# GpSimd takes over part of the scaling of v and of the block sums, and q, k and v get buffers of their own, in a retention layer followed by an MLP

## The chip, the core and the metric

The kernel runs on one core of a Trainium2 chip. The metric is device microseconds for one execution. The core's engines are TensorE (PE; PEld is its loading of weights), VectorE (DVE), ScalarE (ACT), GpSimd (POOL) and SyncE (SP), each of which works through its own list of instructions in order. Loads from memory are issued by GpSimd, stores and transposing copies by SyncE.

## The reference

For 8 sequences of 576 tokens and 8 heads of 64, scores of q and k are weighted by a decay that depends on the head and multiplied with v. The heads are laid side by side (4608 tokens of 512), and an MLP with exact GELU follows.

```
gamma = 1.0 - 2.0 ** (-5.0 - np.arange(H))
Dmat = np.where(rel >= 0, gamma[:, None, None] ** rel, 0.0)
x = matmul((matmul(q, k.T) / sqrt(64)) * Dmat, v)      # then to (B * S, H * D)
h = x @ w_in                                            # 512 -> 2048
g = 0.5 * h * (1.0 + erf(h / sqrt(2)))
out = g @ w_out                                         # 2048 -> 512
```

## The kernel before

**Retention.** The tokens are cut into 36 units of 128 tokens, numbered 0 to 35 (`units`, L138 on). Two sequences go together; a sequence has four chunks of 128 and a tail of 64, and the two tails share a unit. Units 0 to 3 are the first chunks of the first four sequences, and for them and some others v is also used as it was loaded. For each unit q, k and v are loaded (`load_unit`, L504), q and k are turned on PE (the first ten units) or by a transposing DMA (`turn_dma`, L603), PE makes the scores (sc), DVE masks them (ret), and PE multiplies with v scaled by the decay (vh). A running state in PSUM (u_ps, copied to u_sb) carries what earlier chunks contribute. DVE multiplies the result (o_ps) by the decay of the row (dqT) and writes it to x (tile xT, L843 and L855). `scaled_v` (L814) makes vh: on DVE as one product of v_ld with a broadcast of dv (L821), on ACT as eight activations, one for each head (L824). The list VH_ACT (L174) names the units for ACT; the rest go to DVE.

**MLP.** Nine blocks of 512 tokens, so four units each. w_in and w_out are loaded as eight tiles each (wi0 to wi7, wo0 to wo7). The first product goes through a block in four quarters. A quarter is either *plain* (16 matmuls with 512 columns) or a *unit of seven products* (28 matmuls with 256 columns, L1129): seven products of sums of blocks in place of eight products of blocks. LAYOUTS (L192) lists it for blocks 2 to 8: '0' is a unit of quarter 0, '12' two units whose products alternate, 'p3' a plain quarter, '1p2' a unit and a plain quarter that alternate. PRODUCTS (L199) is the order of the seven. A unit needs sums of x (xs, five for each block, `x_sum`, L1046 to 1054) and of w_in (wi_sum), and afterwards four DVE operations that put its quadrants together. In blocks 0 and 1 all is plain, block 0 in pieces of 128 columns. The second product is made of seven products in blocks 1 to 8 (`fast`, L1146) and needs sums of g (tiles s and g, four for each half of a block, `g_sum`, L989 to 999), numbered 0 to 3; the product called 6 needs sum 1, which needs sum 0.

**The order of the work.** No scheduler of the compiler is used. `Plan` (L30) holds operations with an engine, a duration, what they depend on, and a due time, and steps forward in planned time: on each engine it takes the operation that can start first, and among those within a little slack the one due first (`best`, L87). So the instructions of each engine are laid down in an order that is fixed at build time; on the chip only semaphores hold them. Matmul pieces of the MLP are taken from a window of LOOK pieces (L190) of the current product (`pe_candidates`, L1543), and the retention's work is put between them in groups ("macros", L1408); GAP_A, HOLD, APART, BEFORE, LEAD, SPREAD and EASE steer when. APART is read in ALONE (L874) and for groups from the fourth on. A change between tile shapes on PE costs some 0.09 us going in and 0.11 to 0.13 us coming out (start of the last matmul to start of the next, beyond a matmul's own pace).

**Loads.** GpSimd issues the loads in the order ORDER (L196; q3 is q of unit 3), then q, k and v unit by unit. A pair of units shares a slot: one tile for q and k, one for v, four slots in all (N_LD, L169; `tiles_of`, L475). `Ring` (L263) tells the plan when the next slot is free: it sorts the times at which slots were given back (`read`, L494). q, k and v of unit 0 come as float32 by SyncE and ACT. `warm` matmuls (L1515) keep PE busy in the first 16 us.

Of the kernel before, what the change touches and what calls it, by code (L numbers as in the profile page):

```python
# [29 lines left out]
class Plan:  # L30
# [4 lines left out]
    def __init__(self):  # L35
        self.ops = {}
        self.T = dict.fromkeys(self.ENGINES, 0.0)
        self.open = {e: [] for e in self.ENGINES}

# [42 lines left out]

    def start(self, op, engine):
        t = max(self.T[engine], op.ready)
        return max(t, op.at()) if op.at else t
# [13 lines left out]
    def run(self, op, engine, start):  # L99
        op.ran = engine  # L100
        self.T[engine] = self.T["now"] = start + self.dur(op, engine)
        if op.fn:
            op.fn(engine) if op.engine == "any" else op.fn()
        self.done(op, self.T[engine])
# [3 lines left out]
def kernel(  # L108
# [52 lines left out]
    def slot_of(i):  # L161
# [7 lines left out]
    N_LD = 4  # L169
# [4 lines left out]
    VH_ACT = [5, 8, 12, 14, 15, 17, 19, 20, 26, 28, 30, 31, 32, 35, 37]  # L174
# [10 lines left out]
    GAP_A = 4.2  # L185
    GAP_B = 1.5
    APART = [3, 6, 7]
    BEFORE = 0.4
    UNIT_FROM = 2
    LOOK = 16  # L190
    HOLD = 4.6
    LAYOUTS = {2: ['0', '12', 'p3'], 3: ['01', '2', 'p3'], 4: ['2', '30', 'p1'], 5: ['01', '2', 'p3'], 6: ['10', '2', 'p3'], 7: ['01', '23'], 8: ['3', '20', 'p1']}  # L192
    LEAD = 8
    SPREAD = 7.1
    EASE = 6.5
    ORDER = ("q3 q2 k3 q1 pos v2 k2 wi0 k1 wi4 v3 v1 wi1 wi3 wi5 v4 wi2 wi6 k4 wi7 q4 wo0 q5 k5 v5 wo4 wo1 q9 q8 "  # L196
             "wo5 v7 wo6 k7 wo7 v10 wo2 q6 v6 k6 wo3 q7 k10 q10 k8 k9 v9 v8").split()
    K_ORDER = [0, 1, 8, 9, 2, 3, 10, 11, 4, 5, 12, 13, 6, 7, 14, 15]
    PRODUCTS = "3251647"  # L199
# [6 lines left out]
    ld_pool = ctx.enter_context(tc.tile_pool(name="ld", bufs=N_LD))  # L206
# [56 lines left out]
    class Ring:  # L263
        def __init__(self, size):
            self.size, self.taken, self.free = size, 0, []

        def at(self):
            n = self.taken - self.size
            return 0.0 if n < 0 else (sorted(w.end + 0.12 if isinstance(w, Landing) else w for w in self.free)[n] if n < len(self.free) else NEVER)

        def take(self):
            self.taken += 1

        def give(self, when):
            self.free.append(when)

    ld_ring, tr_ring, vh_ring, ret_ring, x_ring = Ring(N_LD), Ring(N_QKT), Ring(N_VH), Ring(N_RET), Ring(3)
# [194 lines left out]
    loaded, slots, w_in_sb, w_out_sb = {}, {}, {}, {}  # L472
    touched = {}

    def tiles_of(i):  # L475

        if i not in loaded:
            n = slot_of(i)
            if i in kept:
                loaded[i] = (const.tile([128, 2, H, D], BF16, name=f"qk_ld{i}"), const.tile([128, H, D], BF16, name=f"v_ld{i}"))  # L480
                return loaded[i]
            if n not in slots:
                ld_ring.take()
                slots[n] = (ld_pool.tile([128, 2, H, 2, D], BF16, tag="qk", name="qk_ld"),
                            ld_pool.tile([128, 2, H, D], BF16, tag="v", name="v_ld"))
            qk, v_ld = slots[n]
            j = units[i][2] or 0
            if i in old:
                loaded[i] = (qk.rearrange("p a (j h) b d -> p j a (h b) d", j=2)[:, j], v_ld[:, j])
            else:  # L490
                loaded[i] = (qk[:, :, :, j], v_ld[:, j])
        return loaded[i]

    def read(i, what):  # L494

        n = slot_of(i)
        got = touched.setdefault(n, set())
        got.add((i, what))
        want = {(m, x) for m in pair_with(i) for x in
                ["v"] + (["turn0", "turn1"] if i < N_PE_TR else ["turn"]) + (["state"] if units[i][1] < NCI - 1 else []) + (["inner"] if i in raw else [])}  # L500
# [1158 lines left out]
```

## Time and profile before

| what | value |
|---|---|
| runs of the kernel before | median 283.02 us (282.54 to 283.83, 3 runs) |
| the profiled execution | 282.72 us, of which the span is 280.7 us |
| granted TensorE clock | 1.00 |
| DVE, ACT, POOL busy | 230.1, 174.0, 110.4 us |
| first matmul of the MLP's first product without warm matmuls behind it | 15.81 us |
| last matmul ends | 276.1 us |

The span runs from the first instruction to the last; some 2 us lie around it. In the page's second part each digit is the busy share of a fortieth of the span, in tenths. A row of instructions names the line, engine, operation and tiles (out<-in), the shapes, the count, then busy time and mean ns of one, then how long the engine sat idle before them and what ended it. A duration contains the tail in which the next instruction has already begun: DVE operations of 0.69 us start 0.60 us apart when nothing holds them. Of the waits the columns are: who waited for whom, us in total, times, the longest. In a timeline the columns are start, duration (of the merged run of instructions), engine, line, operation, tiles and count.

### The profile page before, as it was taken

To read this page: it belongs to the slowest core of one execution; us is meant where nothing else is said; L and a number is where in the kernel's file an instruction comes from. 1 tells how busy PE (TensorE), PEld (TensorE's weight loads), DVE (VectorE), ACT (ScalarE), POOL (GpSimd) and SP (SyncE) were. 2 spreads that over 40 slices of the span, in tenths; PEclk is the share of its full clock that TensorE was granted. 3 is DMA by queue.
4 is the path that set the end of the run, shared out by engine and by line. 5 is a ranking of instruction groups with operands and counts; after the bars stand their busy time and mean duration, and the time that the engine had idled before them with its cause. 6 is when DMAs were issued, how large, how long until landed. Compare 5 with 4: busy or idle time off the path is not lost.

```text
span 280.7 us, 8896 instructions
## 1 busy us (share of the span) xinstructions
PE 273.9 (98%) x3731; PEld 220.0 (78%) x3731; DVE 230.1 (82%) x438; ACT 174.0 (62%) x414; POOL 110.4 (39%) x139
## 2 busy tenths in 40 slices
PE   7999999999999999999999999999999999999993
PEld 2679767578888688868887888688868888888782
DVE  5870465699999998999799999987987799969832
ACT  7678733646438952995297319852898379528740
POOL 8967778847546086233326804705000000000000
PEclk9999999999999999999999999999999999999999
DMA  9999999999999999999989999999800040022013
GB/s 148 165 182 186 178 186 165 142 238 133 127 139 173 197 114 128 140 230 145 156 188 57 134 112 172 210 117 135 184 22 2 6 149 2 4 75 77 0 40 112
DMA packets 152071, 35.57 MB, mean 127 GB/s; under 512 B 141024, under 2 KB 147680, under 8 KB 152032
## 3 DMA queue, kind: packets, MB, share of 16 engines
q0 software_dynamic: 115792, 17.97, 98.1%
q1 hardware_dynamic: 35200, 16.78, 34.9%
q8 instruction: 29, 0.48, 0.8%
q10 hardware_dynamic: 1040, 0.26, 0.4%
q14 instruction: 10, 0.08, 0.1%
HBM read 36.70 MB, written 9.44 MB: 164 GB/s over the span
## 4 chain that ended last, share of the span: by engine, by line
PE 87%; DVE 4%; POOL 4%; DMA 3%; issue 1%; ACT 0%; POOLq 0%; DVEq 0%
PE oT L229 39%; PE hT L229 16%; PE zT L229 10%; PE yT L229 7%; PE o_ps L229 4%; DMA w_in<-in_moe_w_in_dram 3%; PE sc L229 2%; POOL qk_ld L517 2%; PE u_ps L229 2%; DVE s L999 1%; PE qk_ps L233 1%; DVE ret L652 1%; POOL v_ld L517 1%; POOL w_in L523 1%; DVE g L999 0%
## 5 line engine op out<-in xcount | busy, mean ns | idle before, releaser
L229 PEld LDWEIGHTS <-g 128*128 128x128 bf16 x576 | 55.1, 98 | 12.5 <-issue 0.2
L229 PEld LDWEIGHTS <-w_in 128*128 128x128 bf16 x656 | 53.0, 98 | 13.3 <-DMA w_in<-in_moe_w_in_dram 0.4
L229 PE MATMUL hT<-xT,w_in 128*128 128x128 bf16 (+2 forms) x480 | 53.5, 266 | 0.3 <-DMA w_in<-in_moe_w_in_dram 0.3
L229 PEld LDWEIGHTS <-wi_sum 128*128 128x128 bf16 x440 | 42.8, 98 | 6.6
L1099 ACT ACTIVATE g<-hT 128x512 bf16<-128x512 f32 (+1 forms) x72 | 35.9, 505 | 19.5 <-PE hT L229 17.7
L229 PE MATMUL oT<-w_out,g 128*128 128x256 bf16 (+1 forms) x320 | 45.6, 294 | 0.0
L517 POOL DMA_DIRECT2D qk_ld<-in_q_dram x31 | 28.0, 905 | 35.1 <-DMA qkT<-qk_ld 22.8
L229 PEld LDWEIGHTS <-s 128*128 128x128 bf16 x384 | 36.8, 98 | 5.6 <-DVE s L999 0.5
L517 POOL DMA_DIRECT2D v_ld<-in_v_dram x31 | 28.1, 910 | 22.8 <-ACT vh L824 9.5
L229 PE MATMUL oT<-w_sum,s 128*128 128x256 bf16 x256 | 32.4, 273 | 0.2 <-ACT o_sb L1243 0.2
L824 ACT ACTIVATE vh<-v_ld,dv 128x64 bf16<-128x64 bf16 x112 | 31.2, 346 | 1.0 <-DMA v_ld<-in_v_dram 1.0
L229 PE MATMUL oT<-w_sum,g 128*128 128x256 bf16 x256 | 30.8, 273 | 0.0
L517 POOL DMA_DIRECT2D qk_ld<-in_k_dram x31 | 28.0, 903 | 5.5 <-DMA v_ld<-in_v_dram 5.2
L1243 ACT COPY o_sb<-oT 128x512 f32<-128x512 f32 (+1 forms) x27 | 14.5, 538 | 25.2 <-PE oT L229 13.3
L1212 ACT ACTIVATE g<-zT 128x512 bf16<-128x512 f32 x44 | 25.9, 614 | 0.1
L652 DVE TENSOR_TENSOR ret<-sc,msk 128x512 bf16<-128x512 f32 x36 | 23.2, 687 | 1.4 <-PE sc L229 1.4
L1247 DVE TENSOR_TENSOR o_sb<-o_sb,oT 128x512 f32<-128x512 f32 (+1 forms) x27 | 16.8, 629 | 8.8 <-PE oT L229 4.5
L570 ACT COPY q<-yT 128x512 f32<-128x512 f32 x18 | 10.3, 594 | 21.8 <-PE yT L229 21.8
L855 DVE TENSOR_TENSOR xT<-o_ps,dqT 128x512 bf16<-128x512 f32 x26 | 16.8, 686 | 3.3 <-PE o_ps L229 3.3
L821 DVE TENSOR_TENSOR vh<-v_ld,dv 128x512 bf16<-128x512 bf16 x22 | 15.0, 688 | 3.4 <-DMA v_ld<-in_v_dram 3.4
L1221 DVE TENSOR_TENSOR zT<-q,zT 128x512 f32<-128x512 f32 x22 | 15.3, 695 | 1.0 <-PE zT L229 0.6
L1191 DVE TENSOR_TENSOR q<-q,zT 128x512 f32<-128x512 f32 x22 | 14.5, 684 | 1.7 <-PE zT L229 0.8
(170 smaller groups left out, 453.6 us busy)
## 6 DMA issues: line engine op xcount, KB each, us to landing
out_dram<-o_sb SPq DMA_DIRECT2D x30, 256.0 KB, 3.9
qk_ld<-in_q_dram POOLq DMA_DIRECT2D x31, 128.0 KB, 7.6
qk_ld<-in_k_dram POOLq DMA_DIRECT2D x31, 128.0 KB, 8.5
v_ld<-in_v_dram POOLq DMA_DIRECT2D x31, 128.0 KB, 8.0
w_in<-in_moe_w_in_dram POOLq DMA_DIRECT2D x8, 256.0 KB, 8.6
w_out<-in_moe_w_out_dram POOLq DMA_DIRECT2D x8, 256.0 KB, 7.8
out_dram<-o_sb SPq DMA_DIRECT2D x12, 128.0 KB, 2.7
v_ld<-in_v_dram POOLq DMA_DIRECT2D x8, 64.0 KB, 6.4
```

The source lines that it names most:

```text
L229: return nc.tensor.matmul(*args, **more)
L517: nc.gpsimd.dma_start(dst, src[2 * bp + j, :, ci * C:ci * C + C, :].rearrange("h s d -> s h d"))
L652: nc.vector.tensor_tensor(r, t, by, op=ALU.mult)
L821: nc.vector.tensor_tensor(vh, loaded[i][1], dv[:, :, ci:ci + 1].to_broadcast([128, H, D]), op=ALU.mult)
L824: nc.scalar.activation(vh[:, h], loaded[i][1][:, h], AF.Copy, scale=dv[:, h, ci:ci + 1])
L855: nc.vector.tensor_tensor(dst, o, dqT[:, :, ci * C:ci * C + C], op=ALU.mult)
L1099: nc.scalar.activation(g_of(t, m0)[:, m0 % 2:m0 % 2 + n, m0 // 8, lo:hi], hT, AF.Gelu)
L1191: nc.vector.tensor_tensor(q_, q_, chain[key]["Z"][1], op=ALU.subtract)
L1212: nc.scalar.activation(target(key, what), chain[key][n][1], AF.Gelu)
L1221: nc.vector.tensor_tensor(to, chain[key]["q"], z, op=ALU.add)
L1243: nc.scalar.copy(target(key, what), chain[key][n][1])
L1247: nc.vector.tensor_tensor(to, to, chain[key][n][1], op=ALU.add)
```

## The change

- `scaled_v` can run on GpSimd, as the same tensor product as on DVE. VH_POOL lists 19 numbers for it, VH_ACT shrinks from 15 to 4.
- XS_POOL lists 21 of the sums of x (block * 5 + number of the sum) and GS_POOL 20 of the sums of g (block * 8 + half * 4 + number) for GpSimd. The plan counts 1.1 us for v and for a sum of x there, 2.1 us for a sum of g, and a signal that is 0.25 us late (0.12 on DVE).
- The plan lets those operations with two inputs in SBUF (PAIR) of DVE and GpSimd start only when the other engine's last one has ended. This shapes the order alone; nothing on the chip waits for it.
- q, k and v have pools of their own with 3, 5 and 4 slots. A slot of q is given back when q is turned, one of k when the state has read it too. The ring follows the slot that is handed out next, in turn, rather than the first that comes free.
- The parameters of the order are others: the layouts (21 units of seven products and 7 plain quarters in blocks 2 to 8; before 22 and 6), the order of the products and of the loads, and the numbers that steer the groups.

The core of the diff (`read` and the lines that only pass on the new names are left out):

```diff
--- before.py
+++ after.py
@@ -36,6 +36,7 @@
         self.ops = {}
         self.T = dict.fromkeys(self.ENGINES, 0.0)
         self.open = {e: [] for e in self.ENGINES}
+        self.port = {"dve": 0.0, "pool": 0.0}
...
+    PAIR = ("vh", "gs", "xs", "ui", "ws", "dq")
+
     def start(self, op, engine):
         t = max(self.T[engine], op.ready)
+        if engine in self.port and op.name.startswith(self.PAIR):
+            t = max(t, self.port["pool" if engine == "dve" else "dve"])
         return max(t, op.at()) if op.at else t
 
...
+        if engine in self.port and op.name.startswith(self.PAIR):
+            self.port[engine] = self.T[engine]
...
-    N_LD = 4
+    N_LD = {"q": 3, "k": 5, "v": 4}
...
-    VH_ACT = [5, 8, 12, 14, 15, 17, 19, 20, 26, 28, 30, 31, 32, 35, 37]
+    VH_ACT = [8, 12, 22, 23]
+    VH_POOL = [5, 6, 7, 10, 13, 14, 15, 17, 18, 19, 20, 24, 28, 29, 31, 33, 34, 35, 37]
+    XS_POOL = [10, 13, 15, 18, 19, 23, 25, 26, 28, 29, 30, 31, 32, 33, 34, 35, 39, 40, 41, 42, 43]
+    GS_POOL = [18, 24, 25, 27, 33, 36, 39, 45, 46, 48, 49, 52, 53, 56, 57, 58, 63, 65, 67, 71]
     HOT = 10.1
     N_WARM = 8
     SLACK = 0.3
...
-    GAP_A = 4.2
+    GAP_A = 1.0
     GAP_B = 1.5
-    APART = [3, 6, 7]
-    BEFORE = 0.4
+    APART = [6, 7]
+    BEFORE = 0
     UNIT_FROM = 2
-    LOOK = 16
-    HOLD = 4.6
-    LAYOUTS = {2: ['0', '12', 'p3'], 3: ['01', '2', 'p3'], 4: ['2', '30', 'p1'], 5: ['01', '2', 'p3'], 6: ['10', '2', 'p3'], 7: ['01', '23'], 8: ['3', '20', 'p1']}
+    LOOK = 14
+    HOLD = 2.2
+    LAYOUTS = {2: ['2', '30', 'p1'], 3: ['0', '1p2', 'p3'], 4: ['01', 'p2', 'p3'], 5: ['01', '2', 'p3'], 6: ['01', '23'], 7: ['01', '23'], 8: ['0', '1', '2', 'p3']}
     LEAD = 8
-    SPREAD = 7.1
-    EASE = 6.5
-    ORDER = ("q3 q2 k3 q1 pos v2 k2 wi0 k1 wi4 v3 v1 wi1 wi3 wi5 v4 wi2 wi6 k4 wi7 q4 wo0 q5 k5 v5 wo4 wo1 q9 q8 "
-             "wo5 v7 wo6 k7 wo7 v10 wo2 q6 v6 k6 wo3 q7 k10 q10 k8 k9 v9 v8").split()
+    SPREAD = 7.5
+    EASE = 9
+    ORDER = ("pos q2 q3 k2 q1 k3 k1 v2 v3 wi0 v1 wi4 wi1 wi5 wi2 v4 wi6 wi3 wo0 q4 wi7 q5 k5 k4 v5 wo4 v7 wo1 wo5 "
+             "v6 wo6 k6 v10 wo7 k7 q7 wo2 q9 wo3 q6 q8 k10 q10 k9 k8 v9 v8").split()
     K_ORDER = [0, 1, 8, 9, 2, 3, 10, 11, 4, 5, 12, 13, 6, 7, 14, 15]
-    PRODUCTS = "3251647"
+    PRODUCTS = "3251476"
     SECOND = "1267534"
     LAYOUT = {t: ["p0", "p1", "p2", "p3"] for t in range(2, N_BLK)}
     for t in range(UNIT_FROM, N_BLK):
         LAYOUT[t] = LAYOUTS[t]
...
-            self.size, self.taken, self.free = size, 0, []
+            self.size, self.taken, self.free = size, [], {}
 
         def at(self):
-            n = self.taken - self.size
-            return 0.0 if n < 0 else (sorted(w.end + 0.12 if isinstance(w, Landing) else w for w in self.free)[n] if n < len(self.free) else NEVER)
-
-        def take(self):
-            self.taken += 1
-
-        def give(self, when):
-            self.free.append(when)
-
-    ld_ring, tr_ring, vh_ring, ret_ring, x_ring = Ring(N_LD), Ring(N_QKT), Ring(N_VH), Ring(N_RET), Ring(3)
+            n = len(self.taken) - self.size
+            w = self.free.get(self.taken[n], NEVER) if n >= 0 else 0.0
+            return w.end + 0.12 if isinstance(w, Landing) else w
+
+        def take(self, key=None):
+            self.taken.append(len(self.taken) if key is None else key)
+
+        def give(self, when, key=None):
+            self.free[len(self.free) if key is None else key] = when
+
+    ld_ring = {what: Ring(N_LD[what]) for what in "qkv"}
+    tr_ring, vh_ring, ret_ring, x_ring = Ring(N_QKT), Ring(N_VH), Ring(N_RET), Ring(3)
...
+    def slot_for(what, i):
+
+        n = slot_of(i)
+        if (what, n) not in slots:
+            ld_ring[what].take(n)
+            slots[what, n] = ld_pool.tile([128, 2, H, D] if what == "v" else [128, H, 2, D], BF16, tag=what, name=f"{what}_ld", bufs=N_LD[what])
+        return slots[what, n]
+
+    def loaded(what, i):
+
+        if i in kept:
+            if (what, i) not in slots:
+                slots[what, i] = const.tile([128, H, D], BF16, name=f"{what}_ld{i}")
+            return slots[what, i]
+        t, j = slot_for(what, i), units[i][2] or 0
+        if what == "v":
+            return t[:, j]
+        if i in old:
+            return t.rearrange("p (j h) b d -> p j (h b) d", j=2)[:, j]
+        return t[:, :, j]
+
...
-            def fits(i=i):
-                return max(room_to_fly(), 0.0 if i in kept or slot_of(i) in slots else ld_ring.at())
+            def fits(what=what, i=i):
+                return max(room_to_fly(), 0.0 if i in kept or (what, slot_of(i)) in slots else ld_ring[what].at())
...
     def scaled_v(i, engine, heads=(0, H)):
         ci = units[i][1]
         if "vh" not in st[i]:
-            vh_ring.take()
+            vh_ring.take(i)
             st[i]["vh"] = vh_pool.tile([128, H, D], BF16, tag="vh", name="vh")
         vh = st[i]["vh"]
-        if engine == "dve":
-            nc.vector.tensor_tensor(vh, loaded[i][1], dv[:, :, ci:ci + 1].to_broadcast([128, H, D]), op=ALU.mult)
+        if engine != "act":
+            (nc.vector if engine == "dve" else nc.gpsimd).tensor_tensor(
+                vh, loaded("v", i), dv[:, :, ci:ci + 1].to_broadcast([128, H, D]), op=ALU.mult)
         else:
             for h in range(*heads):
-                nc.scalar.activation(vh[:, h], loaded[i][1][:, h], AF.Copy, scale=dv[:, h, ci:ci + 1])
+                nc.scalar.activation(vh[:, h], loaded("v", i)[:, h], AF.Copy, scale=dv[:, h, ci:ci + 1])
         if heads[1] == H:
             read(i, "v")
 
...
+        if i in VH_POOL:
+            add(f"vh{i}", "pool", 1.1, before, lambda i=i: scaled_v(i, "pool"), due, 0.25, at=room)
+        elif i in VH_ACT:
...
-    def g_sum(t, two, which):
+    def g_sum(t, two, which, engine):
...
-        nc.vector.tensor_tensor(out_, x0, x1, op=op)
+        engine.tensor_tensor(out_, x0, x1, op=op)
...
-    def x_sum(t, which):
+    def x_sum(t, which, engine):
...
-        nc.vector.tensor_tensor(xs_tiles[t][:, which], x0, x1, op=op)
+        engine.tensor_tensor(xs_tiles[t][:, which], x0, x1, op=op)
...
-                add(f"gs{t},{two}.{which}", "dve", 0.6, gl + ([f"gs{t},{two}.{which - 1}"] if which else []),
-                    lambda t=t, two=two, which=which: g_sum(t, two, which),
-                    begins["p", t, "5673"[which]] - 1.5 + 0.6 * two,
+                on_pool = t * 8 + two * 4 + which in GS_POOL
+                add(f"gs{t},{two}.{which}", *(("pool", 2.1) if on_pool else ("dve", 0.6)), gl + ([f"gs{t},{two}.{which - 1}"] if which else []),
+                    lambda t=t, two=two, which=which, e=nc.gpsimd if on_pool else nc.vector: g_sum(t, two, which, e),
+                    begins["p", t, "5673"[which]] - 1.5 + 0.6 * two, 0.25 if on_pool else 0.12,
...
-                add(f"xs{t}.{which}", "dve", 0.335, [f"x{i}" for i in range(4 * t, 4 * t + 4)] + ([f"xs{t}.0"] if which else []),
-                    lambda t=t, which=which: x_sum(t, which), soon - 3.0 + 0.1 * which, at=xs_ring.at if not which else None)
+                on_pool = t * 5 + which in XS_POOL
+                add(f"xs{t}.{which}", *(("pool", 1.1) if on_pool else ("dve", 0.335)),
+                    [f"x{i}" for i in range(4 * t, 4 * t + 4)] + ([f"xs{t}.0"] if which else []),
+                    lambda t=t, which=which, e=nc.gpsimd if on_pool else nc.vector: x_sum(t, which, e), soon - 3.0 + 0.1 * which,
+                    0.25 if on_pool else 0.12, at=xs_ring.at if not which else None)
```

## The prediction

> **What bounds the kernel now.** I read the page from the top, then PE's waits, the chain of waits, the timeline of PE and DVE where a block of tokens begins, and the groups of the lines that the change touches.
>
> ```profile
> span 280.7 us, 8896 instructions
> PE 273.9 (98%) x3731; PEld 220.0 (78%) x3731; DVE 230.1 (82%) x438; ACT 174.0 (62%) x414; POOL 110.4 (39%) x139
> ...
> PE   7999999999999999999999999999999999999993
> PEld 2679767578888688868887888688868888888782
> DVE  5870465699999998999799999987987799969832
> ...
> POOL 8967778847546086233326804705000000000000
> PEclk9999999999999999999999999999999999999999
> ```
>
> PE is filled from the first slices to the last, at full clock. A busy PE is not PE at its peak, so its waits come next:
>
> ```profile
> PE warm L229 <- DVE ln_scale L347: 1.2, 1, 1.2
> PE hT L229 <- DMA w_in<-in_moe_w_in_dram: 0.3, 1, 0.3
> PE oT L229 <- ACT o_sb L1243: 0.2, 1, 0.2
> ```
>
> That is all that PE waits for in 280 us. DVE (82%) and ACT (62%) are relieved by this change, but PE hardly waits for them. How much is left on PE is read from starts: in the timeline 256-column matmuls start 0.109 us apart, 512-column ones 0.216 us, and what lies above that is a stall. Where the stall is seen best is the start of block 2:
>
> ```profile
> 81.35 1.31 DVE L855 TENSOR_TENSOR xT<-o_ps,dqT 128x512 bf16<-128x512 f32 x2
> 82.55 1.79 DVE L1054 TENSOR_TENSOR xs<-xT 128x512 bf16<-128x512 bf16 x5
> ...
> 81.26 1.80 PE L229 MATMUL oT<-w_sum,g 128*128 128x256 bf16 x15
> 83.04 0.60 PE L229 MATMUL yT<-xs,w_in 128*128 128x256 bf16 x4
> ```
>
> 15 matmuls from 81.26 fill PE up to 82.90; the next starts at 83.04, behind the first sum of x (82.55 to about 82.98): 0.14 us lost. Gone through like this, PE after 18 us has seven such places that are not a change of tile shape: 0.42 (18.7 us, a w_in tile), 0.12 (72.4), 0.14 (82.9), 0.28 (160.5), 0.14 (161.2), 0.16 (192.4) and 0.14 (242.5): 1.4 us. More than this no faster DVE or ACT can give back after 18 us.
>
> **The change part by part.**
>
> *PE's own work.* The new layouts hold 21 units and 7 plain quarters instead of 22 and 6. A unit is 28 matmuls of 256 columns, 28 x 0.109 = 3.06 us; a plain quarter is 16 of 512 columns, 16 x 0.216 = 3.46 us. So **+0.4 us** on an engine with no cover. The same 28 pieces of the second product remain in each block. APART loses its 3, but the list is read only for groups from 4 on, and group 3 is in ALONE anyway since group 2 is not fine: 0 us, no change of tile shape is saved.
>
> *Work moved.* The rows:
>
> ```profile
> L824 ACT ACTIVATE vh<-v_ld,dv 128x64 bf16<-128x64 bf16 x112 | 31.2, 346 | 1.0 <-DMA v_ld<-in_v_dram 1.0
> L821 DVE TENSOR_TENSOR vh<-v_ld,dv 128x512 bf16<-128x512 bf16 x22 | 15.0, 688 | 3.4 <-DMA v_ld<-in_v_dram 3.4
> L1054 DVE TENSOR_TENSOR xs<-xT 128x512 bf16<-128x512 bf16 x35 | 12.8, 424 | 0.0
> L999 DVE TENSOR_TENSOR s<-g 128x1024 bf16<-128x1024 bf16 x16 | 10.9, 687 | 0.0
> L368 POOL IOTA val<- 128x128 f32 x1 | 0.2, 237 | 0.4 <-POOLq L1643 0.4
> ```
>
> There are 36 units of v, numbered 0 to 35, so the 37 in the new list (as in the old) names none: GpSimd scales 18, ACT 4 (was 112/8 = 14), DVE 14 (was 22). ACT loses 80 activations x 31.2/112 = 22 us. DVE loses 8 x 0.69 + 21 x 0.42 + 20 x 0.69 = 28 us, and with the four operations of one unit less (0.69 each) 31 us. All of that lies beside PE: it buys a share of the 1.4 us, no more. I count half of it, **-0.7 us**, because 0.42 of it is a DMA and the stalls at 72, 192 and 242 us stand where a block's sums are made, which is just where GpSimd comes in.
>
> GpSimd gets 18 + 21 operations on 512 elements and 20 on 1024. The trace has no such operation of it. Below: the iota, 237 ns for 128 elements a partition with nothing read, is 1.85 ns per element, so 0.95 and 1.9 us. Above: three streams (two read, one written) at the iota's rate each, 2.85 and 5.7 us. I take 1.1 and 2.1 us, near the lower end, because the iota is the only row of that engine's arithmetic: 39 x 1.1 + 20 x 2.1 = 85 us. Its row shows 110 us, nearly all DMA issues of 0.7 to 0.9 us and all before 198 us; 195 us in 281 still fits. At the upper end it would be 111 + 114 + 110 = 335 us and would bound the kernel.
>
> *What is queued behind them.* GpSimd issues all loads in order; a sum that waits for its g holds the loads behind it. From 50 us a load takes 6 to 10 us from issue to landing and is asked for well ahead, and no PE wait names such a load: 0 us, and up to the sum's wait (2 us) if that lead is used up.
>
> *The tight sums.* A sum is due when PE takes its first product. The first use of s in block 6 is at 214.16 us; the second half's g is complete near 210.1 and DVE's two sums behind it end at 212.4. On GpSimd both (0 and 1 of half 1) are 2 x 2.1 = 4.2 us, thus ready at about 214.5, and PE's second quarter of that product comes near 215: no slack is left. In block 2 the first sum of x goes to GpSimd where DVE already made PE late: 1.1 instead of 0.45 us. PE may take any of 14 pieces meanwhile, so I count 0.3 us for the one and 0.2 for the other: **+0.5 us**, between 0 and the 3.5 us of the slower rival below.
>
> *The start.* The loads land one after the other from 7.5 us: 10 unit loads and 8 of w_in between 7.50 and 27.21 us, which fits 0.85 and 1.38 us each. In the new order two more unit loads precede wi0: it lands near 14.8 (was 12.81), wi4 near 17.1 (14.94), wi1 18.4 (19.14), wi5 19.8 (21.29), wi2 21.2 (23.53), wi6 23.4, wi3 24.8, wi7 28.4 (27.21). The first block's PE work on one w_in tile is 4 x 0.45 = 1.8 us, more than the 1.38 between tiles, so it stays ahead once four units are ready. Now PE is solid from 15.81, with 1.25 us of attention and the 0.42 us stall still inside and 0.45 us of MLP done: MLP work done at T is T - 17.0. With the new order q, k and v of units 2 and 3 land by 13.6, so three units' pieces on wi0 (1.35 us) can run before wi4 at 17.1, and about 0.55 us of attention is left: T - 16.3. **-0.7 us**, between +0.6 (wi0 2 us later with nothing to fill) and -1.3. GpSimd's iota for pos moves ahead of the first load, 0.32 us; the first three loads, issued 0.9 us apart, land 0.9 us apart behind the fp32 loads that end at 6.62, so I cost it at nothing, else 0.3 us.
>
> *Own buffers for q, k and v.* GpSimd's waits before loads (22.8 us for the transposes, 14.7 + 5.0 for u_ps) shrink. PE waits for none of these loads, so 0 us; nothing comes next behind them either. The end (a last DVE sum at 276.12, then the store) is as before.
>
> Sum: 282.72 (the profiled execution: span 280.7 and 2.0 around it) + 0.4 - 0.7 + 0.5 - 0.7 = **282.2 us**. The median shown is 283.02, 0.3 above that execution; I keep 282.2.
>
> [...]
>
> **The rivals.**
> *Forecast, no measurable change, 0.40*: 281.6 to 284.4.
> *Faster, 0.28*: the new order keeps PE off all seven stalls and the start gives its full 1.3: 282.72 + 0.4 - 1.4 - 1.3 = 280.4; with two thirds of that gain, 281.2. For it: DVE is busy for all of 57 to 85 us and for 26.8 of the 28 us from 139 to 167, where four of the stalls are. Against it: PE's work grew.
> *Slower, 0.20: GpSimd's sums become what PE waits for.* Place: the first sums of a block. In block 7 DVE's second sum of half 0 ends at 239.6 and PE uses s at 239.91; both sums go to GpSimd, 2 x (2.1 - 0.6) = 3.0 us later against 0.3 of slack: 2.7. Block 2's first sum of x: 1.1 and a later signal against 0.45: 0.8. Together 3.5 in place of the 0.5 counted: 285.2. For it: these slacks. Against it: GpSimd has no loads left in block 7 and can begin as soon as g is there. It decides once two such sums end later than the 14 pieces (14 x 0.436 = 6.1 us) that PE can take meanwhile.
> *Slower, 0.12: the two engines hold each other.* DVE keeps two-input instructions of 14 v, 14 x, 44 g and 36 weight sums: 14 x 0.69 + 14 x 0.42 + 44 x 0.69 + 36 x 0.43 = 61 us in 281, while GpSimd would be at work for 85. If such an instruction has to wait for a whole GpSimd one, 1 to 2 us, it costs PE where there is no slack: block 1's second sum ends at 72.0 for a first use at 72.08, block 2's at 82.98 for 83.04, block 7's at 239.6 for 239.91. Three holds of 1 us: 285.2, and up to 3 more if the long ones meet them: 288. In this trace GpSimd's arithmetic ends at 5.3 us and meets no such DVE instruction, so no row speaks for or against it. It decides once a hold is longer than the slack of its place.
> That the change does not do what it says can only be the one unit that does not exist.
>
> Half a per cent, 1.4 us, is about what a measurement of this kernel can tell from no change. Faster 0.28, same 0.40, slower 0.32. The slower chance is that of both slow rivals. The range takes in most of the fast case, the first slow one and the holds of 1 us: 280.8 to 286.2, and leaves out the long holds and the best fast case; the likeliest case alone, 281.6 to 284.4.
>
> **What the profile after would show.** Right: GpSimd's rows for vh and xs near 1.1 us, those for s and g near 2.1; PE's waits still under 1 us after 20 us; the first solid PE stretch near 16 to 17 us; DVE near 200 us busy, ACT near 150. Wrong: PE or PEld waiting for POOL s or xs by microseconds, above all near the starts of blocks 2, 6 and 7; GpSimd operations of 3 us or more; DVE rows with a mean well above 424 and 688 ns, which would be the two engines holding each other.

## The result, and the profile after

The kernel after takes 296.6 us (median of 6 runs, 292.7 to 299.6) beside 282.7 us: ratio **1.0371, 95% interval 1.0336 to 1.0406**. The forecast was no measurable change, 282.2 us with a range up to 286.2. The runs of this kernel fall into two groups, 292.7 to 294.1 and 299.1 to 299.6 us; the ratio is that of the lower group, the profiled execution took 299.1, and I rest nothing on its length alone: the same kernel on another chip (first experiment) shows the same waits. The page, in the lines that were shown of before:

```profile
span 297.3 us, 8800 instructions
...
PE 278.7 (94%) x3715; PEld 219.6 (74%) x3715; DVE 221.0 (74%) x382; ACT 156.8 (53%) x335; POOL 199.4 (67%) x198
...
PE   7989999999999979997299999999999999999993
...
POOL 8957899498379598577335498996747553770530
PEclk9999999999999999999959999999999999999999
```

PE has holes, the deepest in the twentieth slice, and the slice behind it runs at half the clock. GpSimd is now at work to the end. What PE waits for (columns as before: us in total, times, longest):

```profile
PE oT L239 <- POOL s L1024: 7.0, 2, 6.0
PE oT L239 <- POOL g L1024: 1.6, 1, 1.6
...
PE hT L239 <- DMA w_in<-in_moe_w_in_dram: 0.8, 1, 0.8
```

PE waits for GpSimd's sums, and two of GpSimd's rows show the durations that were assumed:

```profile
L842 POOL TENSOR_TENSOR vh<-v_ld,dv 128x512 bf16<-128x512 bf16 x18 | 19.8, 1108 | 0.1
...
L1024 POOL TENSOR_TENSOR s<-g 128x1024 bf16<-128x1024 bf16 x5 | 10.6, 2129 | 16.2 <-ACT g L1237 13.7
```

1.11 and 2.13 us, where 1.1 and 2.1 were taken (its sums of x took 1.22 us, its slowest row of sums of g 2.33). Counted as in the prediction (start to start beyond a matmul's own pace, all above 0.04 us, without the single doubled gaps where the trace lacks a matmul), PE's stalls are 32.9 us for 17.2 before: +15.7 of the 16.6 us by which the span grew. A part of this is a slower PE: half the clock was granted from 147.9 to 154.7 us, at the end of its longest wait and after it. Two things stand behind the waits in the trace.

**The hold.** I call *held* what a DVE operation takes beyond its usual time, that of the operations of its line and shape that meet no GpSimd operation. DVE operations with two inputs in SBUF were held for 19.0 us in all (before: 0.0); those that read PSUM (60 masks, 26 x products and others) for 0.0. From DVE's timeline and GpSimd's:

```profile
133.10 2.25 DVE L1024 TENSOR_TENSOR s<-s,g 128x1024 bf16<-128x1024 bf16 x1
...
132.65 2.14 POOL L1024 TENSOR_TENSOR s<-g 128x1024 bf16<-128x1024 bf16 x1
134.86 2.46 POOL L1024 TENSOR_TENSOR s<-s,g 128x1024 bf16<-128x1024 bf16 x1
```

A sum that takes DVE 0.69 us alone begins inside GpSimd's sum (132.65 to 134.79) and ends at 135.35, 0.55 behind it; GpSimd's next, from 134.86 us, is longer, 2.46.

**The queue**, that is operations in GpSimd's list that stand behind one that waits. GpSimd's timeline, then PE's:

```profile
138.63 0.91 POOL L538 DMA_DIRECT2D q_ld<-in_q_dram  x1
146.30 0.88 POOL L538 DMA_DIRECT2D k_ld<-in_k_dram  x1 [6.76 <-DMA qkT<-k_ld]
147.20 2.13 POOL L1024 TENSOR_TENSOR s<-g,s 128x1024 bf16<-128x1024 bf16 x1
...
142.76 0.60 PE L239 MATMUL oT<-w_sum,g 128*128 128x256 bf16 x4
149.39 3.60 PE L239 MATMUL oT<-w_out,s 128*128 128x256 bf16 x16 [6.02 <-POOL s L1024]
```

A load of k waits 6.76 us for its buffer, the sum s for block 3 is queued behind it, and PE stands 6.02 us. The next 25 matmuls start 0.213 us apart in place of 0.109: 2.6 us more. The buffer was not free because the tiles are not handed out in turn: in the built program the five k buffers come as A B C D E A B D C E A C B ..., while v's come in turn. The plan's ring assumes turns.

### The profile page after: what moved, and what is told of

Same layout as the page of the kernel before. It is cut to its first block, busy times and chain, and to the rows that moved or that the text cites. A ratio compares the mean times of both kernels' runs of the same rounds, so it can differ in the third digit from the quotient of the medians.

```text
span 297.3 us, 8800 instructions
## 1 busy us (share of the span) xinstructions
PE 278.7 (94%) x3715; PEld 219.6 (74%) x3715; DVE 221.0 (74%) x382; ACT 156.8 (53%) x335; POOL 199.4 (67%) x198
## 5 line engine op out<-in xcount | busy, mean ns | idle before, releaser
L239 PEld LDWEIGHTS <-w_in 128*128 128x128 bf16 x664 | 53.8, 98 | 15.6 <-DMA w_in<-in_moe_w_in_dram 1.0
L239 PE MATMUL hT<-xT,w_in 128*128 128x128 bf16 (+2 forms) x496 | 57.1, 269 | 0.8 <-DMA w_in<-in_moe_w_in_dram 0.8
L1124 ACT ACTIVATE g<-hT 128x512 bf16<-128x512 f32 (+1 forms) x76 | 38.4, 510 | 20.2 <-PE hT L239 18.5
L239 PEld LDWEIGHTS <-wi_sum 128*128 128x128 bf16 x420 | 40.5, 98 | 8.5 <-DVE q L1229 1.6
L538 POOL DMA_DIRECT2D k_ld<-in_k_dram x31 | 28.0, 904 | 11.5 <-DMA qkT<-k_ld 6.8
L1272 DVE TENSOR_TENSOR o_sb<-o_sb,oT 128x512 f32<-128x512 f32 (+1 forms) x27 | 16.6, 625 | 23.3 <-PE oT L239 14.4
L538 POOL DMA_DIRECT2D q_ld<-in_q_dram x31 | 28.2, 911 | 7.8 <-DMA qkT<-q_ld 6.1
L1079 POOL TENSOR_TENSOR xs<-xT 128x512 bf16<-128x512 bf16 x21 | 25.4, 1225 | 7.9 <-DVE xT L877 7.0
L1268 ACT COPY o_sb<-oT 128x512 f32<-128x512 f32 (+1 forms) x27 | 14.4, 539 | 30.2 <-PE oT L239 15.4
L1024 POOL TENSOR_TENSOR s<-s,g 128x1024 bf16<-128x1024 bf16 x7 | 16.0, 2284 | 15.2 <-DVE s L1024 14.9
L673 DVE TENSOR_TENSOR ret<-sc,msk 128x512 bf16<-128x512 f32 x36 | 22.7, 680 | 0.8 <-PE sc L239 0.8
L239 PE MATMUL oT<-w_out,s 128*128 128x256 bf16 x128 | 17.5, 291 | 6.0 <-POOL s L1024 6.0
L1024 POOL TENSOR_TENSOR s<-g 128x1024 bf16<-128x1024 bf16 x5 | 10.6, 2129 | 16.2 <-ACT g L1237 13.7
L842 POOL TENSOR_TENSOR vh<-v_ld,dv 128x512 bf16<-128x512 bf16 x18 | 19.8, 1108 | 0.1
```

The lines of the kernel that those rows point to most:

```text
L239: return nc.tensor.matmul(*args, **more)
L538: nc.gpsimd.dma_start(loaded(what, i), src[2 * bp + j, :, ci * C:ci * C + C, :].rearrange("h s d -> s h d"))
L673: nc.vector.tensor_tensor(r, t, by, op=ALU.mult)
L842: (nc.vector if engine == "dve" else nc.gpsimd).tensor_tensor(vh, loaded("v", i), dv[:, :, ci:ci + 1].to_broadcast([128, H, D]), op=ALU.mult)
L1024: engine.tensor_tensor(out_, x0, x1, op=op)
L1079: engine.tensor_tensor(xs_tiles[t][:, which], x0, x1, op=op)
```

## The experiments

All ratios are to the kernel before on the same chip. *Held* is DVE's; *stalls* are PE's as counted above, 17.2 before. Both columns shift by up to 1 and 2 us with where the usual duration and the pace are set, so only larger differences are read from them. Of the 18 kernels two are small ones of their own. e5 has two runs, the others of the table four or more.

| kernel | us | ratio, 95% interval | held | stalls |
|---|---|---|---|---|
| after, again (e1) | 298.3 | 1.0553, 1.0507 to 1.0598 | 18.6 | 30.6 |
| after, buffers in turn (e2) | 297.1 | 1.0486, 1.0447 to 1.0526 | 24.1 | 31.8 |
| after, sums of g made by DVE, order kept (e3) | 289.3 | 1.0248, 1.0202 to 1.0294 | 10.5 | 22.7 |
| after, all made by DVE, order kept (e4) | 291.4 | 1.0310, 1.0291 to 1.0330 | 0.0 | 25.6 |
| old order, GpSimd's lists (e5) | 298.2 | 1.0549, 1.0489 to 1.0610 | 15.6 | 34.5 |
| old order, own buffers, empty lists (e6) | 286.1 | 1.0123, 1.0089 to 1.0157 | 0.0 | 20.2 |
| the same, buffers in turn (e17) | 283.9 | 1.0056, 1.0025 to 1.0087 | 0.0 | 18.0 |
| new order, empty lists (e7) | 285.2 | 1.0091, 1.0073 to 1.0109 | 0.0 | 18.7 |
| the same, buffers in turn (e9) | 284.8 | 1.0078, 1.0063 to 1.0093 | 0.0 | 19.9 |
| only v on GpSimd (e10) | 286.4 | 1.0138, 1.0117 to 1.0159 | 6.3 | 21.3 |
| only x (e11) | 286.9 | 1.0152, 1.0126 to 1.0179 | 3.1 | 22.1 |
| only g (e12) | 297.8 | 1.0538, 1.0496 to 1.0580 | 16.8 | 34.8 |
| only g, blocks 6 to 8 (e13) | 284.7 | 1.0071, 1.0056 to 1.0086 | 5.4 | 20.0 |
| only g, blocks 2 to 5 (e14) | 298.4 | 1.0548, 1.0483 to 1.0613 | 13.2 | 33.5 |
| empty lists, idle sums beside (e15) | 301.2 | 1.0647, 1.0605 to 1.0689 | 15.6 | 34.7 |
| all but g of blocks 2 to 5 (e18) | 289.1 | 1.0237, 1.0189 to 1.0286 | 15.4 | 23.0 |

From e5 on, where lists differ, the plan laid the order anew for those lists.

### Hold or queue: four kernels with the plan's order kept

The first is the kernel after, unchanged, on another chip. In the second the tiles are used in turn:

```diff
-            slots[what, n] = ld_pool.tile(...)
+            slots[what, n] = own[what, (len(ld_ring[what].taken) - 1) % N_LD[what]]
```

In the third the sums of g, and in the fourth every operation of GpSimd, are emitted on DVE at the same place of the same order:

```diff
-  e=nc.gpsimd if on_pool else nc.vector: g_sum(t, two, which, e)
+  e=nc.vector: g_sum(t, two, which, e)
```

> The changed kernel once more, for a second trace of it. Queue theory (a load that waits in GpSimd's list stands in front of a sum of g): the trace has a PE wait of 1 us or more whose sum of g lies behind a waiting load; 292 to 300 us. Hold theory (DVE and GpSimd exclude each other where both read two tensors in SBUF): DVE rows of s, g, xs, vh, w_sum, wi_sum are lengthened by 15 to 20 us in all, those that read PSUM by nothing, in this trace too.

> The changed kernel with fixed tiles for the slots of q, k and v that are really used in turn; the plan and every engine's order stay. Queue theory: the load of k behind the third tail no longer waits for the tail's transposes, so the 6.2 us PE wait near 143 us and the slow clock behind it go: 6 to 9 us less than the first trace of the changed kernel, 288 to 291. Hold theory: the DVE rows stay lengthened by 15 to 20 us and the time stays at 292 or more.

> The changed kernel with its 20 sums of g on DVE, at the same place of the same plan; v and x stay on GpSimd. Queue theory: no sum of g stands behind a load, 10 us of PE waits go: 285 to 289. Hold theory: the long holds (2.1 us) go, those of 1.1 us stay, so DVE is lengthened by 5 to 9 us in place of 19 and the time falls by 2 to 4 us only: 289 to 291.

> The changed kernel with all 58 operations of GpSimd on DVE, at the same place of the same plan, which is 28 us more work for DVE than the plan counts. Queue and hold theories together: no hold and no sum behind a load, so what is left is the new order: 283 to 286. Rival, the new order and buffers themselves are bad or DVE is now too full: 288 or more, with PE waiting for DVE.

Measured: with the buffers in turn the 6.8 us wait of the k load is gone, and the time is hardly less (the intervals overlap). PE still stood 3.8 us at that place (5.7 in the first kernel), for a hold; from the second kernel's DVE timeline:

```profile
138.69 4.92 DVE L1087 TENSOR_TENSOR xs<-xT 128x512 bf16<-128x512 bf16 x1
```

A sum of x, 0.42 us alone, takes 4.92: GpSimd issued loads from 138.27 to 140.08, then made a sum of g to 142.22 and one of x to 143.32. It was held through all of that, though in the kernel before, where GpSimd issues loads and makes no sums, such operations were held for 0.0 us. And at 87 us PE stood 2.7 us that it did not stand in the first kernel: three sums of x took DVE 3.90 us there, beside two loads and a sum of x on GpSimd. So **the queue theory failed as the whole account**: its wait was real, and taking it away uncovered holds that cost nearly as much. Without the sums of g the loss halves, although DVE then has 14 us of work that the order does not count. With everything on DVE no operation is held; the ratio is 1.031, of which 0.9% is the new order by itself (e7, below), so this kernel says what 28 us of uncounted DVE work cost and little of the hold.

### Order and buffers without GpSimd's arithmetic

e5 has the old layouts, load order and steering numbers with the new GpSimd lists; e6 the old ones with empty lists; e7 the new ones with empty lists (e6 and e7 with the old VH_ACT):

```diff
-    VH_POOL = [5, 6, 7, ...]
-    XS_POOL = [10, 13, 15, ...]
-    GS_POOL = [18, 24, 25, ...]
+    VH_POOL = XS_POOL = GS_POOL = []
```

> The code of the changed kernel with the old layouts, load order and steering numbers, but with the new lists for GpSimd (units that neither list names as before: ACT 5, DVE 13), planned anew. Hold theory: DVE is lengthened by 15 us or more here too and PE waits for it: 292 or more, whatever the order. Order theory (the new order has no slack, the move itself is harmless): 283 to 286.

> The code of the changed kernel with the old order and empty lists for GpSimd: what is left of the change are the buffers of q, k and v and the ring that counts them in turn. If these are harmless: 282 to 284. If the out-of-turn buffers of k hurt by themselves: loads come late and PE waits for q, k or v, 285 or more.

> The changed kernel with empty lists for GpSimd and the old list for ACT, planned anew: the new layouts, load order and buffers alone. PE's work is 0.4 us more and the start lost 0.4 in the traces. If hold and queue are the whole loss: 283 to 286. If the order is bad in itself: 288 or more.

> The kernel without any GpSimd arithmetic in the new order (285.2 us, ratio 1.009, before it), with the buffers of q, k and v made fixed tiles that are really used in turn, as the plan assumes. If the buffers handed out otherwise than planned are what the new order and the own buffers cost, the time falls to 283.5 us or less (ratio 1.003 or less). If the cost lies in the order itself (one more unit of seven products in place of a quarter without them, +0.4 us, and loads that the new order brings later), nothing changes: 284.8 to 285.6 us. It computes the reference in full.

> The old order with own buffers and without GpSimd arithmetic (ratio 1.0123), with fixed buffers really used in turn. If the buffers handed out otherwise than planned cost the 1.2%, the ratio falls to 1.004 or less. If not (in the new order the same edit moved 1.0091 to 1.0078, within the intervals), it stays at 1.009 to 1.014, and the cost lies in the order that the new account of the buffers makes.

Measured: GpSimd's lists cost about the same in the old order (1.0549) as in the new one, so the new order is not what makes them cost. The own buffers and the new ring, alone, cost 1.2%; used in turn, 0.6%. So about half of that is buffers handed out otherwise than planned, between the two cases expected; in the new order the same edit changes nothing that the intervals can tell. The new order without GpSimd is 0.9% slower than before.

### Which operations: v, x, g, early g, late g

Each keeps one of the lists (those without v on GpSimd have the old VH_ACT); e13 keeps of GS_POOL the numbers from 48 (blocks 6 to 8, 11 sums, where no load is issued any more), e14 those below 48 (9 sums). e18 is the kernel after without those nine.

```diff
-    GS_POOL = [18, 24, 25, 27, 33, 36, 39, 45, 46, 48, 49, 52, 53, 56, 57, 58, 63, 65, 67, 71]
+    GS_POOL = [18, 24, 25, 27, 33, 36, 39, 45, 46]
```

> The kernel after, planned anew, with GpSimd's scalings of v alone (18 operations of 1.1 us; the 41 sums are on DVE). Hold theory: in the kernel after, 85 us of GpSimd work brought 19 us of longer DVE operations and, against the same order without GpSimd work, some 12 us of time, so 0.14 us for each us; 20 us give +2.8 us over 285.2: 288. Rival (only a sum behind a waiting load costs): no sum is on GpSimd, and a scaling has slack of microseconds, so 285 to 286. DVE's operations with two SBUF inputs longer by about 4 us by the hold theory, and that alone is no proof of lost time.

> The kernel after, planned anew, with GpSimd's 21 sums of x alone (24 us of it). Hold theory: +3.4 us over 285.2: 288.6. Rival (only a sum of g behind a waiting load costs): 285 to 286; sums of x that stand behind a waiting load would show as PE waiting for GpSimd's xs.

> The kernel after, planned anew, with GpSimd's 20 sums of g alone (43 us of it). Hold theory: +6 us over 285.2: 291. Rival (only sums behind a waiting load cost, and these are the sums of g): it carries nearly the whole difference, +10 to +12 us, 295 to 297. If neither alone costs its share (the three parts sum to much less than 12 us), the cost comes from GpSimd's queue being full: operations behind one another and behind loads.

> The kernel with the 20 sums of g alone (ratio 1.054; 1.009 without them), with only those 11 of them that belong to blocks 6 to 8, where no load stands in GpSimd's queue any more. Queue theory: they cost next to nothing, ratio 1.007 to 1.014. Hold theory, and the theory of the sum's own length (2.13 us for 0.69 on a chain of four): both are as large there as early, so 11/20 of the loss, ratio 1.03 to 1.035.

> Only the 9 sums of g of blocks 2 to 5, which stand among loads in GpSimd's queue. Queue theory: nearly the whole loss, ratio 1.04 to 1.054, with PE waiting for a sum that stood behind loads. Hold or length alone: 9/20 of it, ratio about 1.03.

> The kernel after, planned anew, with only the nine sums of g of blocks 2 to 5 given back to DVE; GpSimd keeps the 18 scalings of v, the 21 sums of x and the 11 late sums of g. If the early sums carry the loss, what is left is the sum of the parts measured alone: 1.009 without any, +0.005 for v, +0.006 for x, -0.002 for the late sums: ratio 1.018, so 287.8 us. If many GpSimd operations beside DVE cost by their number, 50 of the 59 are left and the ratio is 1.04 or more.

Measured, against 1.0091 without any: v and x cost 0.5 and 0.6% each, far less than their share of GpSimd's time; the 20 sums of g cost 4.5%; and of these **the nine early ones cost all, the eleven late ones nothing** (1.0071). A price for each us of GpSimd's work fails on v and x (288 and 288.6 us were expected, 286.4 and 286.9 came) and on g (291, and 297.8 came). The hold theory's 1.03 for both early and late sums missed twice, while the queue theory's ranges, 1.007 to 1.014 and 1.04 to 1.054, met the one and came within 0.1% of the other. But in the kernel with the early sums PE waits for GpSimd only once for long, 2.2 us; the other three long waits, 2.1, 2.0 and 2.0 us, are for DVE. And the late sums are held too. In the kernel with the late ones, DVE, then PE:

```profile
214.32 1.94 DVE L1024 TENSOR_TENSOR s<-g,s 128x1024 bf16<-128x1024 bf16 x1
216.18 2.60 DVE L1024 TENSOR_TENSOR g<-g 128x1024 bf16<-128x1024 bf16 x1
...
216.07 0.60 PE L239 MATMUL oT<-w_sum,s 128*128 128x256 bf16 x4
216.51 1.04 PE L239 MATMUL oT<-w_sum,g 128*128 128x256 bf16 x8
```

Two DVE sums take 1.94 and 2.60 us, and PE goes on: it has matmuls that need neither. For each GpSimd sum DVE is held for 5.4/11 = 0.5 us late and for 13.2/9 = 1.5 us early: the late ones hold it less, and here PE had other work. In the kernel with the early ones, GpSimd, DVE, PE:

```profile
99.95 0.88 POOL L538 DMA_DIRECT2D v_ld<-in_v_dram  x1 [0.39 <-DMA q_ld<-in_q_dram]
100.84 2.13 POOL L1024 TENSOR_TENSOR g<-g 128x1024 bf16<-128x1024 bf16 x1
...
100.49 3.04 DVE L1024 TENSOR_TENSOR s<-g,s 128x1024 bf16<-128x1024 bf16 x1
103.45 0.68 DVE L673 TENSOR_TENSOR ret<-sc,msk 128x512 bf16<-128x512 f32 x1
...
104.18 1.91 PE L239 MATMUL oT<-w_sum,s 128*128 128x256 bf16 x16 [1.98 <-DVE ret L673]
```

DVE's sum begins at 100.49, while GpSimd still issues the load in front of its own sum, and is held to 103.53; the mask `ret`, which reads PSUM and takes its usual 0.68 us, stands behind it, and PE waits for that.

With the early sums back on DVE the ratio is 1.0237, for 1.018 expected from the parts: just above, so some 0.6% more comes from v, x and the late sums together. A part of it is the queue: at 114 us PE waits 1.4 us for a sum of x behind a load that had waited 2.2 us; the rest stays unexplained. Of the kernel after's loss it gives back more than half by the second measurement (1.0553) and a third by the first (1.0371). It also shows that held time is no price by itself: DVE is held for 15.4 us here and for 13.2 with the early sums alone, which lose more than twice as much.

### Sums that nobody waits for

In the kernel without GpSimd arithmetic, beside each of the same 20 sums, GpSimd makes two half sums of the same g into tiles that are read no more:

```diff
+        if t * 8 + two * 4 + which in BESIDE:
+            for n, what in enumerate("qk"):
+                nobody = slots[what, min(kept)].rearrange("p (a h) d -> p a (h d)", a=2)
+                nc.gpsimd.tensor_tensor(nobody, a21[:, 2 * n:2 * n + 2], a22[:, 2 * n:2 * n + 2], op=op)
         engine.tensor_tensor(out_, x0, x1, op=op)
```

> The kernel without GpSimd arithmetic (ratio 1.009), where beside each of the same 20 sums, which DVE makes itself, GpSimd makes two sums of half the size (1.1 us each) of the same g into a tile that nobody reads: 40 more operations, with no one waiting for them; the result is the reference's. Hold theory: DVE's sums are held as in the kernel with the 20 sums (some 15 us of longer DVE operations), and PE waits for them: ratio 1.025 to 1.045. Queue or length theory: nobody waits for GpSimd's sums, so 1.009 to 1.014; loads come some 2 us later each time, which the loads' slack should take.

Measured: 1.0647, more than the real sums cost, and more than either theory expected. No one waits for GpSimd's results here; only DVE waits twice, 1.0 us each, until GpSimd has read a g that DVE then overwrites. From DVE's timeline and PE's:

```profile
100.37 3.56 DVE L1030 TENSOR_TENSOR s<-g,s 128x1024 bf16<-128x1024 bf16 x1
...
105.18 2.08 PE L239 MATMUL oT<-w_sum,s 128*128 128x256 bf16 x9 [3.10 <-DVE ret L673]
```

The same place as above, the same held sum, the same `ret`, and 3.1 us of PE. At another place no load stands directly ahead of the two half sums; GpSimd, DVE, PE:

```profile
167.15 1.53 POOL L1029 TENSOR_TENSOR q_ld<-g 128x512 bf16<-128x512 bf16 x1 [1.29 <-DVE g L1030]
168.65 1.59 POOL L1029 TENSOR_TENSOR k_ld<-g 128x512 bf16<-128x512 bf16 x1
...
167.59 1.64 DVE L1030 TENSOR_TENSOR s<-g,s 128x1024 bf16<-128x1024 bf16 x1
169.16 1.63 DVE L842 TENSOR_TENSOR vh<-v_ld,dv 128x512 bf16<-128x512 bf16 x1
...
172.04 1.38 PE L239 MATMUL oT<-w_sum,g 128*128 128x256 bf16 x7 [3.00 <-DVE ret L673]
```

Two holds of 0.95 us are most of PE's 3.00. And at 228 us, where all loads are done, PE waits 1.98 us for a sum on DVE that stands behind held ones, so late sums are not harmless as such.

From 95 us on, that is beside all of the idle sums, PE's waits name DVE for 10.2 us (`ret` 6.1, s 3.3, xT 0.8) and no load; the 43 matmuls at half the clock behind two of these waits add 4.4 (the mean granted clock of this execution was 0.979, in e7 1.000). Together that is 14.6 of the 16.0 us by which PE's stalls grew against e7 (34.7 for 18.7). So **the hold is enough** for a loss of this size, but for the 2.1 us in which DVE waits for g; that PE waits for GpSimd's long sums, or for what is queued on GpSimd, is not needed. That does not say what share each has in the kernel after, where they lie on top of one another.

### The hold by itself

Two small kernels, which compute nothing of the reference and write zeros. In the first, stages of DVE operations of 512 elements beside GpSimd sums of 512 or 1024; in the second beside GpSimd's fills, its DMA issues, and sums with an issue ahead of each.

> A kernel of its own that leaves the whole computation out, writes zeros and measures the hold: VectorE operations on 512 elements beside sums, loads or nothing on GpSimd. Hold theory: DVE operations with two inputs in SBUF (0.41 us alone) last up to 1.5 us beside sums of 512 and up to 2.6 us beside sums of 1024, and get longer the more GpSimd operations follow each other; beside loads alone they keep 0.41; with one input in PSUM they keep 0.69 beside the same sums. Rival, GpSimd and DVE merely share bandwidth: all of them get slower by a common factor, PSUM ones too.

> A small kernel of its own that writes zeros and leaves the whole computation out. It sets DVE operations beside GpSimd's fills (which read nothing), beside DMA issues, and beside sums with a DMA issue ahead of each. [...] DVE sums of float32 with two SBUF inputs are held as the bf16 ones are. Open: whether a sum with a DMA issue ahead of it holds DVE from the issue on, some 3 us in all, as 2.56 us in an earlier run suggests; if the issue holds nothing, 2.3 us at most.

| DVE operation, us alone | beside GpSimd | us |
|---|---|---|
| two bf16 inputs in SBUF, 0.41 | sums of 512 (1.15 alone) | 1.37 |
| the same | sums of 1024 (2.11 alone) | 2.33 |
| one input in PSUM, 0.69 | sums of 1024 | 0.69 |
| bf16 copy, 0.28 | sums of 1024 | 2.20 |
| two bf16 inputs, 0.41 | fills (0.95 alone) | 0.41 |
| bf16 copy, 0.28 | fills | 1.11 |
| two inputs, one float32, 0.68 | sums of 1024 | 2.60 |
| two bf16 inputs, 0.41 | DMA issues, one behind the other | 0.41 |
| bf16 copy, 0.28 | DMA issues | 0.65, one in three |

Beside the six sums of 1024, the first from 54.75 to 57.04 us, DVE began seven operations with two bf16 inputs up to 66.4 us, 2.06 us each on average and the first of them ahead of the sums: one for each sum, and it ended behind that sum (57.32 us for the first). Operations with one input in PSUM were not held by such sums (18 in 10.86 us, 0.69 each); beside fills, which read nothing, those with two bf16 inputs kept their 0.41 us and the copies did not. None of these stages shows what the last one does, GpSimd's timeline and DVE's:

```profile
78.19 0.91 POOL L69 DMA_DIRECT2D ld<-in_v_dram  x1
79.12 2.13 POOL L61 TENSOR_TENSOR gp<-a,gate 128x1024 bf16<-128x1024 bf16 x1
81.18 0.91 POOL L69 DMA_DIRECT2D ld<-in_v_dram  x1
82.12 2.13 POOL L61 TENSOR_TENSOR gp<-a,gate 128x1024 bf16<-128x1024 bf16 x1
...
78.33 6.68 DVE L46 TENSOR_TENSOR dv<-a,gate 128x512 bf16<-128x512 bf16 x1
```

One operation of 0.41 us takes **6.68 us**: through an issue, a sum, a second issue and a second sum. The expectation (some 3 us) was less than half of it. The next one took 2.60. So the issue in front of a sum need not be a gap in which DVE gets its turn. Sometimes it is one: during the fourth issue (87.17 to 88.08) three operations went through in 0.41 us each, and only the next met the sum (2.33). What decides between the two is not shown.

## Why the prediction was wrong

*The step that failed: the sum has no term for the two engines' hold.* It was left at nothing because no row of the trace before spoke for or against it, and it stood only in a rival of 0.12 with the price **"Three holds of 1 us"** and up to 3 more. The runs show instead 18 held operations of up to 2.6 us in the kernel after, 19.0 us in all with the small ones, and up to 4.92 us where loads are issued in between (e2; 3.04 in e14, 3.56 in e15); and in e15, where nobody uses what GpSimd makes, PE's stalls still grow by 16 us. So the rival of 0.12 was right in its mechanism, and in its condition, "once a hold is longer than the slack of its place"; too low were the number of holds and their length. It also looked only at the sum of x or g that is held: much of PE's wait comes from the mask queued behind it (6.1 of 10.2 us in e15).

*Work moved, −0.7 ("a share of the 1.4 us, no more").* The sign of the whole move was wrong. DVE did get relief (221.0 us busy less 19.0 held is 202, forecast about 200; ACT 156.8, about 150), but PE's stalls rose by 15.7 us. No gain from work that lies beside PE can be seen, and the engine it went to held DVE for 19.0 us.

*The tight sums, +0.5, and the first slow rival (block 2, 6, 7).* The places were chosen by slack before a first use, for s late in the kernel; there GpSimd's sums alone cost nothing (1.0071 for 1.0091). The loss from the sums of g stood in blocks 2 to 5, among loads and attention work, of which the step had looked at one sum of x only.

*"A sum that waits for its g holds the loads behind it", 0 to 2 us.* The direction that mattered was the other: a load that waits holds the sum behind it, 6.02 us of PE at one place. Taking that wait away gained nothing measurable, since holds lay under it (e2).

*Own buffers at 0.* They cost 1.2% in the old order, 0.6% once used in turn. The step looked only at who waits for the loads now, not at what the program hands out and how the plan's order changes with it.

*The start, −0.7.* The same later event, the first scores of the next group, comes at 33.04 us for 32.67, so 0.4 us later and not 0.7 earlier; the wait for w_in grew from 0.42 to 1.0 us.

*PE's own work, +0.4, and the durations* held: the first product's row is 57.1 us (496 matmuls) without GpSimd in the new order, 53.5 us (480) before, a plain quarter of 16 more; GpSimd's operations took 1.11 us for v, 1.22 for x and 2.13 to 2.33 for g. For the durations this was partly luck: they were scaled from one iota's 1.85 ns an element, and the same trace has another of 5 elements a partition that took 322 ns.

*Still open:* how the loss of the kernel after divides between hold, queue and length; how much of the early sums' cost is the issues ahead of them and how much the missing slack (e15 shows that a hold can cost PE without an issue directly ahead); what makes the new ring's remaining 0.6%. No version here beat the kernel before. None has the loads off GpSimd's queue, so early sums with no load in that queue were not measured.

## What to carry to other kernels

Before work moves to GpSimd, count not what it relieves but which DVE operations with two SBUF inputs (or SBUF copies) stand beside it (beside sums of 1024 elements, 0.41 us became 2.33 here, and a copy's 0.28 became 2.20), and what is queued behind those: a mask that PE needs pays for a sum that nobody hurried for. Where GpSimd also issued the loads, one hold lasted through a whole sequence of issues and operations (4.92 us in e2, 6.68 in the small kernel); price that, not one operation. Try such a move in pieces by place, early and late, since sums that were harmless in one stage here (1.0071) carried the whole loss in another (1.0548).

## What the runs showed of the hardware

- A DVE operation with two inputs in SBUF that met a GpSimd sum with a DMA issue ahead of it was held from within the issue on, and through the next issue and sum too: 6.68 us for 0.41 in the small kernel; in e2 it was 4.92 for 0.42, through two issues and two sums. It was not always so: three of 0.41 us passed during another such issue. Beside issues alone it took 0.41.
- GpSimd's sums were longer too: one of 1024 elements took 2.29 us in place of 2.11 beside held DVE operations in the small kernel, 2.46 in the kernel after (at 134.86 us) and in e12 (at 131.81 us).
- After PE had stood for 6.18 us, its next 25 matmuls started 0.213 us apart in place of 0.109 (2.6 us more); after 3.26 us in e15 the next nine took 2.08 us, where nine take 1.15 in the kernel before, and the loss was 2.7 us in all. After 3.64 us in e12 the next eight ran at full pace (1.05 us), and half the clock was granted from 136.1 to 143.0 us, from within a second wait of 2.2 us. In e14 half the clock (137.5 to 140.9 us) followed two waits of 2.4 and 2.2 us with eight matmuls between them. So in these four the length of the last wait alone does not tell whether the clock falls.
